# Maxima tasks in pairs at even distances, the first maxima rows through GpSimd's queue, and a second buffer for retrieved rows in a two-branch attention kernel

## Chip, core and metric

The kernel runs on one core of a Trainium2 chip. The metric is the device time of one execution in microseconds (us); the kernel before was run three times, and its median is 1981.27 us (1977.9 to 1982.19).

## The reference, cut to what matters

One input x of 2048 tokens and 512 features goes through two attention blocks of 32 heads of 16 columns each, and a gate mixes the two results.

```python
def _A_ref(x, wq, wk, wv, wo, beta):         # 4 segments of 512 tokens
    ...
    for s in range(N):
        qs, ks, vs = q[:, :, s], k[:, :, s], v[:, :, s]
        logits = einsum("bhqd,bhkd->bhqk", qs, ks) * scale + mask
        a_dot = einsum("bhqk,bhkd->bhqd", softmax(logits), vs)
        num = einsum("bhld,bhde->bhle", phi(qs), M)
        den = einsum("bhld,bhd->bhl", phi(qs), z)[..., None] + 1e-6
        outs.append(g * (num / den) + (1.0 - g) * a_dot)
        M = M + einsum("bhld,bhle->bhde", phi(ks), vs)
        z = z + einsum("bhld->bhd", phi(ks))
    ...
def _B_ref(x, wqkv, wo):                     # plain attention over all 2048 tokens
    ...
x = A_x
g = sigmoid((x * gate_w).sum(-1, keepdims=True))
return g * _A_ref(...) + (1 - g) * _B_ref(...)
```

Block A attends within a segment (its mask adds -1e9 where the key stands ahead of the query) and adds what a memory M, z of the earlier segments retrieves; block B has no mask.

## The kernel before

The program has a projection stage, an attention stage and a short tail. An attention unit is four heads and 512 queries; there are 32 units of B and 32 of A, and step k of the attention stage works on unit 32+k (B) and unit k (A) together.

**Projection.** Every product with a weight is a job of twelve 128x512 matmuls, because each operand is split into a high and a low part and three of the four products are kept. `qk_job` (L279) makes one 128-column group of Q or K for 512 tokens. ScalarE and VectorE split its PSUM bank into a tile `st` of four buffers (L286, L289), and two transfers store it to DRAM (L295). For block A, VectorE and ScalarE also make phi from the same bank (L285, L288, L291), so such a bank comes free only after the last of these. `v_job` (L262) makes V.

The part that the change touches is a loop over 16 blocks `blk`, group g and segment c of block A. A block runs two jobs of A (Q and K), then the memory of A: `mem_tr` transposes phi(K), `mem_upd` adds it to the state (L350, L358, L359), `mem_out` retrieves rows for Q, and `mem_put` transposes these and stores them. In between stand jobs of B from a list `fill`. From block 4 on these share four PSUM banks (`TB` twice, `MB`, `PVB`); another two (`SBK`, 128x1024 each) belong to the maxima.

**Retrieved rows.** `mem_out` copies two PSUM banks with ScalarE into a tile `om` (L314), VectorE scales it (L316 to L320), `mem_put` transposes it on TensorE (L327), ScalarE copies the result back into the same `om` (L329), and SyncE's queue stores it (L331). `om` has one buffer, so the next `mem_out` can't write it before that store has landed.

**Maxima.** The softmax subtracts a bound per query, which needs the maximum of the scores. `s_b` (B) and `s_a` (A) are maxima tasks. One is a pair of matmuls on the two 64-row halves of the array (L449 for B; L427 with mask matmuls L431 for A) into one of the two `SBK` buffers in turn, and one VectorE reduction of that buffer (L451; L435, L437). Unit 32 has 32 tasks and unit 0 six; these 38 are the list `first`. They are issued between the projection jobs by `spill()`, which is called after most pieces of a block. Blocks 4 to 13 each add 3.8 to a quota, and each call takes one task while the quota is at least 1, so a block's tasks stand behind its first pieces, one at a time. In block 14 the first six tasks of unit 33 (`EARLY`) follow in the same way; their keys have just been loaded into the space of x (tile `xh`, L148 and L369).

**From maxima to attention.** `m_chain(0)` (L460 to L470, VectorE) joins the maxima, `m_rows(0)` in block 15 transposes them (L476), ScalarE copies them to the tile `mr` (L478), and four small transfers (L484) write them into rows 48, 49, 112 and 113 of the query tiles of unit 32 (`qb`) and unit 0 (`qa`). The first score matmuls of the attention stage (L503, `t_group`) read these rows. The exponentials of L503's banks are L509, the products with V are L525. `m_rows` is called again in each step for the next units.

**Order.** Each engine runs its instructions in the order of the program. Nearly all transfers are issued by SyncE's queue (SP), one after another, and each waits there for its own data; weights and constant rows are issued by GpSimd's (POOL).

Of the kernel before, what the change touches and what calls it, by code (L numbers as in the profile page):

```python
# [7 lines left out]
FT = mybir.dt.float32  # L8
# [10 lines left out]
E = 16  # L19
# [8 lines left out]
S_FIRST = 10  # L28
S_LAST = 10
OMI = 14  # L30


@with_exitstack
def gated_mix_kernel(ctx, tc, x, wq, wk, wv, wo, beta, wqkv, wob, gate_w, out):
    nc = tc.nc
# [35 lines left out]
    X = proj.enter_context(tc.tile_pool(name="proj", bufs=1))  # L71
# [23 lines left out]
    def misc():  # L95
        return bank(mode["misc"])
# [48 lines left out]
    def set_aux(t, a, eng=None):  # L145
        n = t.shape[1] // 64
        for j in range(2):
            (eng or nc.gpsimd).dma_start(t.bitcast(FT)[64 * j + 48:64 * j + 64].rearrange("r (n t) -> r n t", n=n),  # L148
                                         aux[:, a, None, :].to_broadcast([E, n, 64]))
# [86 lines left out]
    def split_wv(k):  # L236
        split(WV[0][:, k, :], WV[1][:, k, :], WR.pop(k))
# [63 lines left out]
    def mem_state(g, c):  # L301
        return MST[c % 2][g % 2]

    def mem_out(g, c):
        m = mem_state(g, c)[:, :, :E + 1]
        o = X.tile([128, 4, 8, E], FT, name="om")
        r = X.tile([128, 4, 8], FT, name="recm")
        for n in range(2):
            b = misc()[:, :16 * (E + 1)].rearrange("p (i h e) -> p i h e", i=2, h=8)
            for i in range(2):  # L310
                nc.tensor.matmul(b[:, i], PHI[g, 0, c][:, (2 * n + i) * 128:(2 * n + i + 1) * 128], m,
                                 start=True, stop=True)
            nc.scalar.activation(r[:, 2 * n:2 * n + 2], b[:, :, :, E], AF.Copy)
            nc.scalar.activation(o[:, 2 * n:2 * n + 2].rearrange("p i h e -> p (i h) e"),  # L314
                                 b[:, :, :, :E].rearrange("p i h e -> p (i h) e"), AF.Copy)
        nc.vector.tensor_scalar(r, r, 1e-6, None, op0=OP.add)  # L316
        nc.vector.reciprocal(r, r)
        nc.vector.tensor_tensor(r, r, gate[:, 4 * c:4 * c + 4, None].to_broadcast([128, 4, 8]), op=OP.mult)
        o3 = o.rearrange("p i h e -> p (i h) e")
        nc.vector.tensor_tensor(o3, o3, r.rearrange("p i h -> p (i h)")[:, :, None].to_broadcast([128, 32, E]), op=OP.mult)  # L320
        PHI[g, "o", c] = o
# [53 lines left out]
    def q_of(u):  # L375
        return QA[u % 2] if u < 32 else QB[u % 3]
# [95 lines left out]
    def m_rows(k):  # L472
        m8 = M8.pop(k)
        b = misc()[0:64, :128]
        for a in range(2):
            nc.tensor.matmul(b[32 * a:32 * a + 32], m8[:, a], ident, start=True, stop=True)  # L476
        mr = W.tile([64, 128], FT, name="mr", bufs=1)
        nc.scalar.activation(mr, b, AF.Copy)  # L478
        for n, u in ((1, 32 + k if k < 32 else None), (0, (0, None)[k] if k < 2 else k - 1)):
            for a in range(2):  # L480
                if u is None:
                    continue
                r = 32 * a + 16 * n
                nc.sync.dma_start(q_of(u).bitcast(FT)[48 + a:128:64], mr[r:r + 16])  # L484

    PT = {}
    AT = {}
# [148 lines left out]
    ST_B = [(i, p, kc) for i in range(4) for p in range(2) for kc in range(4)]  # L636
    ST_A = [(3, 0), (3, 1), (2, 0), (2, 1), (1, None), (0, None)]

    def s_tasks(u):
        return [todo(s_a, u, *t) for t in ST_A] if u < 32 else [todo(s_b, u, *t) for t in ST_B]  # L640
# [60 lines left out]
    first = s_tasks(32) + s_tasks(0)  # L701
    st33 = [todo(s_b, 33, *t) for t in sorted(ST_B, key=lambda t: t[2])]
    early = st33[:EARLY]
# [6 lines left out]
    split_wv(2)  # L710
    nf = 0
    quota = 0

    def spill():
        nonlocal quota
        if quota >= 1:
            quota -= 1
            (first or early).pop(0)()

    S0 = [b[:, 0] for b in SBK]  # L720
    CUM = (2, 4, 6, 9, 11, 13, 16, 18, 20, 22, 24, 27, 29, 32, 34, 36)
    for blk in range(16):
        g, c = divmod(blk, 4)
        pg, pc = divmod(blk - 1, 4)
        if blk == 4:
            mode["misc"] = TB + [MB, PVB]
        if 4 <= blk < 14:
            quota += len(ST_A + ST_B) / 10
        if blk == 14:
            for p in range(2):  # L730
                set_aux(KB[1][:, p], 0, nc.sync)
            load_kb(1, 0)
        n = blk + 1 + (c == 2)
        if c < 3 and n < 16:
            load_vm(n // 4, n % 4)
        qk_job(0, "A", g, 0, c)
        if c == 3 and g < 3:
            split_w(0, "A", g + 1, (0,))
        spill()
        if blk == 0:  # L740
            split_wv(3)
            do_beta()
        if blk > 0:
            if pc == 0:
                mem_upd(pg, pc)
        qk_job(0, "A", g, 1, c)
        spill()
        if c == 2 and g < 3:
            load_w("A", g + 1)
        if c == 3 and g < 3:  # L750
            split_w(0, "A", g + 1, (1,))
        if blk == 4:
            load_q(33)
            load_ka(0)
            load_q(0)
            load_va(0)
        if blk == 6:
            load_w("B", 1)
        for f, n in ((store_gate, 5), (load_grow, 7), (do_grow, 10)):
            if blk == n:  # L760
                f()
        if blk == 14:
            m_chain(0)
        if blk == 15:
            m_rows(0)
        want = CUM[blk]
        mt = [[], [], []]
        if c > 0:
            mt[0] += [todo(mem_out, g, c)]
            mt[2] += [todo(mem_put, g, c)]  # L770
        if c < NC4 - 1:
            mt[1 + (c == 0)] += [todo(mem_tr, g, c)]
        for n in range(3):
            for f in mt[n]:
                f()
            if blk == 14 and n == 2:
                quota = EARLY
            if mt[n]:
                spill()
            if blk == 14:  # L780
                load_kb(1, 1 + n)
            if nf == 35:
                mode["misc"] = [MB, PVB, TB[1]]
            if nf < want:
                fill[nf]()
                spill()
                if nf in (18, 24):
                    load_w("B", 2 + nf // 24)
                if nf in (15, 20, 26):
                    split_w(2 if nf == 20 else 1, "B", nf // 5 - 2)  # L790
                nf += 1
        if blk == 13:
            for f in first:
                f()
            first, quota = [], 0
        if 0 < c < NC4 - 1:
            mem_upd(g, c)
        if blk == 14:
            spill()
        if blk == 15:  # L800
            for f in early:
                f()
        if nf >= 16 and "vb" not in AT:
            AT["vb"] = 1
            load_vb(0)
# [42 lines left out]
    def extras(k):  # L848
# [5 lines left out]
        post[2 * S_LAST + 4] = [todo(m_rows, k + 1)]  # L854
        for n, at in [(k - 9, 1)] + [(23, 2 * OMI)] * (k == 31):
            if n >= 0:
# [99 lines left out]
    for t in range(4):  # L956
        d = den[:, t * 128:(t + 1) * 128]
        o = o_cols(3, t)[:, 3, 0]
# [36 lines left out]
```

## Time and profile before

| what | value |
|---|---|
| median of three runs (lowest, highest) | 1981.27 us (1977.9, 1982.19) |
| profiled execution: span from first to last instruction | 1976.0 us |
| lowest run less this span, highest run less this span | 1.9 us, 6.2 us |
| TensorE busy | 1944.8 us, 98% |
| VectorE busy | 1630.3 us, 83% |
| ScalarE busy | 1435.7 us, 73% |
| GpSimd busy | 257.5 us, 13% |
| mean granted TensorE clock | 0.997 |

The page gives the profiled execution's span, not the time that a timed run of it would show; the two differ by what lies ahead of the first and behind the last instruction. A row of the timeline has the start in us, the length in us, the engine, the line, the operation, what is written <- what is read, the shape and the count of instructions merged into the row; in brackets stands how long the engine was idle before it and what ended that. PE is TensorE's matmuls, PEld its weight loads, DVE VectorE, ACT ScalarE, POOL GpSimd, SPq an issue by SyncE's queue. A row of the windows view has the stretch, its length, the busy us of each engine with instruction counts, the granted TensorE clock, the busy share of the transfer engines, and GB/s.

### The profile page before, as it was taken

Reading aid. Unit: us, or ns where it says so; the run is one execution under the profiler, and the core shown is the slowest. Engines: PE = TensorE matmul, PEld = TensorE weight load, DVE = VectorE, ACT = ScalarE, POOL = GpSimd, SP = SyncE. Lnnn points to the kernel's source line nnn. Section 1 sums busy time; section 2 is a strip of 40 time slices with the busy share of each in tenths; the row PEclk is TensorE's granted clock in tenths of the full one; section 3 lists DMA queues with packets and bytes.
Section 4 is the critical chain, followed back from the end, with each engine's and each line's share of the span. In section 5 each row is a group of like instructions: output and inputs, shape, how many; then the busy total and the mean of one; then the engine's idle time right before and its main releaser. Section 6 shows DMA issues by size and latency. Waiting matters only on the chain.

```text
span 1976.0 us, 43643 instructions
## 1 busy us (share of the span) xinstructions
PE 1944.8 (98%) x17517; PEld 945.6 (48%) x17517; DVE 1630.3 (83%) x1825; ACT 1435.7 (73%) x2703; POOL 257.5 (13%) x474
## 2 busy tenths in 40 slices
PE   8999999999999999999999999999999999999999
PEld 6887777434344344444444444444444444444435
DVE  6135665899999999999999999999999999999942
ACT  3233332688888888888888888888888888888884
POOL 2200000011210101111010101010101010101012
PEclk9999999999999999999999999999999999999999
DMA  6766656644443444344445353444344444444111
GB/s 205 172 209 183 191 186 173 152 111 114 97 114 88 103 86 103 86 114 86 114 85 112 86 113 86 114 86 114 86 108 91 96 102 87 102 90 103 48 51 57
DMA packets 162742, 222.49 MB, mean 113 GB/s; under 512 B 39260, under 2 KB 89452, under 8 KB 156780
## 3 DMA queue, kind: packets, MB, share of 16 engines
q1 hardware_dynamic: 159596, 211.70, 44.0%
q0 software_dynamic: 2944, 8.00, 2.1%
q8 instruction: 138, 2.26, 0.5%
q14 instruction: 64, 0.52, 0.1%
HBM read 148.21 MB, written 68.16 MB: 109 GB/s over the span
## 4 chain that ended last, share of the span: by engine, by line
PE 90%; DMA 3%; DVE 2%; ACT 2%; issue 1%; SPq 1%; ACTq 0%; DVEq 0%
PE pvb L525 31%; PE tb L503 17%; PE sbk L449 12%; PE mb L503 8%; PE tb L279 3%; PE tb L591 2%; PE mb L279 2%; PE sbk L427 2%; PE pvb L279 2%; PE tb L262 2%; DVE mxb L451 1%; ACT raw L509 1%; PE mb L591 1%; PE mb L262 1%; PE sbk L431 1%
## 5 line engine op out<-in xcount | busy, mean ns | idle before, releaser
L451 DVE TENSOR_REDUCE mxb<-sbk 128x2 f32<-128x1024 f32 x1024 | 1226.1, 1222 | 36.6 <-PE sbk L449 32.4
L509 ACT ACTIVATE raw<-tb 128x512 f32<-128x512 f32 x1557 | 888.2, 598 | 163.1 <-PE tb L503 90.7
L525 PE MATMUL pvb<-raw,vb 128*17 128x256 f32 (+1 forms) x8072 | 639.4, 388 | 0.0
L509 ACT ACTIVATE raw<-mb 128x512 f32<-128x512 f32 x780 | 466.4, 598 | 76.5 <-PE tb L503 44.8
L503 PE MATMUL tb<-qb,xh 64*128 64x512 f32 x872 | 330.8, 496 | 1.7 <-ACT raw L509 1.7
L525 PEld LDWEIGHTS pvb<-raw,vb 128*17 128x17 f32 x8072 | 134.4, 95 | 341.7 <-issue 336.6
L449 PE MATMUL sbk<-xh,qb 64*128 64x512 f32 x1344 | 283.1, 398 | 2.0 <-DMA xh<-dB 0.8
L503 PE MATMUL mb<-qb,xh 64*128 64x512 f32 x445 | 219.6, 494 | 0.0
L503 PEld LDWEIGHTS tb<-qb,xh 64*128 64x128 f32 x872 | 124.4, 183 | 188.1 <-issue 91.4
L512 POOL TENSOR_SCALAR_AFFINE_SELECT raw<-raw 128x256 f32<-128x256 f32 (+1 forms) x320 | 116.1, 363 | 700.1 <-ACT raw L509 692.3
L503 PE MATMUL tb<-qb,kb 64*128 64x512 f32 x471 | 176.3, 496 | 1.4 <-DMA qb<-mr 0.8
L435 DVE TENSOR_REDUCE mx<-sbk 128x2 f32<-128x768 f32 (+1 forms) x128 | 139.8, 1092 | 43.1 <-PE sbk L431 37.1
L449 PE MATMUL sbk<-kb,qb 64*128 64x512 f32 x704 | 150.6, 406 | 1.2 <-DVE mxb L451 1.1
L449 PEld LDWEIGHTS sbk<-xh,qb 64*128 64x128 f32 x1344 | 137.9, 186 | 7.3 <-DVE mxb L451 3.5
L503 PEld LDWEIGHTS mb<-qb,xh 64*128 64x128 f32 x445 | 81.3, 183 | 86.6 <-issue 48.0
L503 PE MATMUL mb<-qb,kb 64*128 64x512 f32 x233 | 115.4, 495 | 0.7 <-DVE st L289 0.7
L565 POOL TENSOR_TENSOR o<-o,d 128x512 f32<-128x512 f32 x31 | 39.8, 1283 | 562.6 <-DMA d<-rd 281.6
L503 PEld LDWEIGHTS tb<-qb,kb 64*128 64x128 f32 x471 | 66.0, 183 | 98.4 <-issue 52.5
L525 PE MATMUL pvb<-raw,va 128*17 128x256 f32 (+2 forms) x1280 | 94.7, 383 | 5.8 <-ACT pvs L534 5.8
L427 PE MATMUL sbk<-ka,qa 64*128 64x256 f32 (+3 forms) x512 | 86.8, 346 | 1.2 <-ACT raw L509 1.2
L503 PE MATMUL tb<-qa,ka 64*128 64x384 f32 (+3 forms) x340 | 79.2, 372 | 0.0
L449 PEld LDWEIGHTS sbk<-kb,qb 64*128 64x128 f32 x704 | 71.6, 185 | 12.6 <-issue 6.5
(273 smaller groups left out, 1790.7 us busy)
## 6 DMA issues: line engine op xcount, KB each, us to landing
xh<-dB SPq DMA_DIRECT2D x38, 512.0 KB
vb<-vdB SPq DMA_DIRECT2D x16, 1088.0 KB
dB<-st SPq DMA_DIRECT2D x64, 256.0 KB
dA<-st SPq DMA_DIRECT2D x64, 256.0 KB
pd<-pvs SPq DMA_DIRECT2D x64, 256.0 KB
kb<-dB SPq DMA_DIRECT2D x22, 512.0 KB
xh<-dB SPq DMA_DIRECT2D x38, 256.0 KB
qb<-dB SPq DMA_DIRECT2D x64, 128.0 KB
```

What stands on the lines that cost most here:

```text
L262: nc.tensor.matmul(b, lhs, WV[wi][:, k, :], start=n == 0, stop=n == 11)
L279: nc.tensor.matmul(b, WS[ws][w][wi][:, k, :], (XH, XL)[xi][c][:, k, :], start=n == 0, stop=n == 11)
L427: nc.tensor.matmul(b[:, j, c0:c0 + n], q_of(u)[r, p, i * 128:(i + 1) * 128], k_of(u, p)[r, :n], start=True, stop=False)
L435: nc.vector.tensor_reduce(m[:, :, p, i], b[:, :, :n], axis=AX.X, op=OP.max)
L449: nc.tensor.matmul(b[:, j], q_of(u)[r, p, i * 128:(i + 1) * 128], k_of(u, p)[r, kc * C:(kc + 1) * C], start=True, stop=True)
L451: nc.vector.tensor_reduce(MXB[u][:, :, p, i, kc], b, axis=AX.X, op=OP.max)
L503: nc.tensor.matmul(bs[j][:, c0:c0 + w], k_of(u, h // 2)[r, 128 * it:128 * it + 128], q_of(u)[r, h // 2, q0:], start=True, stop=True)
L509: nc.scalar.activation(pt, bs[j], AF.Exp, scale=SCALE)
L512: nc.gpsimd.affine_select(out=m, in_=m, pattern=[[1, 128]] if n < 2 else [[0, 2], [1, 128]], compare_op=OP.is_ge, fill=0.0, base=0, channe ...
L525: nc.tensor.matmul(PVB[32 * h:32 * h + E + 1, q0 + lo:q0 + hi], vt[:, it, 4 * q + h, :], pt[:, lo:hi], start=it == 0 and lo == 0, stop=it ...
L565: nc.gpsimd.tensor_tensor(o, o, d, op=OP.mult)
L591: nc.tensor.matmul(b, (AT["oh"], AT["ol"])[oi][:, g, a], (AT["wh"], AT["wl"])[wi][:, g, a], start=n == 0, stop=n == 11)
```

## The change

```diff
+SPILLS = 64
...
     def mem_out(g, c):
         m = mem_state(g, c)[:, :, :E + 1]
-        o = X.tile([128, 4, 8, E], FT, name="om")
+        o = X.tile([128, 4, 8, E], FT, name="om", bufs=2)
...
                 r = 32 * a + 16 * n
-                nc.sync.dma_start(q_of(u).bitcast(FT)[48 + a:128:64], mr[r:r + 16])
+                (nc.sync if k else nc.gpsimd).dma_start(q_of(u).bitcast(FT)[48 + a:128:64], mr[r:r + 16])
...
     quota = 0
+    rate = 0
 
     def spill():
         nonlocal quota
-        if quota >= 1:
-            quota -= 1
-            (first or early).pop(0)()
+        quota += rate
+        if quota >= 2:
+            quota -= 2
+            for _ in range(2):
+                (first or early).pop(0)()
...
-        if 4 <= blk < 14:
-            quota += len(ST_A + ST_B) / 10
+        rate = len(ST_A + ST_B) / SPILLS if 4 <= blk < 14 else 0
```

In blocks 4 to 13 every call of `spill()` now adds 38/64 of a task, and two tasks are issued together once the sum reaches 2. The six tasks of block 14 come two to a call. The four writes of `m_rows(0)` are issued by GpSimd's queue; later calls keep SyncE's. `om` has two buffers. Lines below the first added one shift by one (L449 of the kernel before is L450 here, and so on), those behind the new `spill()` by three or four.

What TensorE's queue holds in block 7 (the rows with `sbk` are maxima tasks, `ws` and `wv` are weights, `mst` is the memory state), first as it was:

```order
L449 MATMUL sbk_114<-kb_89,qb_70 128x512 x2
L279 MATMUL pvb<-xh_88,ws_101 128x512 x4
L279 MATMUL pvb<-xh_88,ws_102 128x512 x4
L279 MATMUL pvb<-xl_96,ws_101 128x512 x4
L449 MATMUL sbk_113<-kb_89,qb_70 128x512 x2
L311 MATMUL tb_109<-mst_108,phi_1522 128x136 x2
L311 MATMUL tb_110<-mst_108,phi_1522 128x136 x2
L449 MATMUL sbk_114<-kb_89,qb_70 128x512 x2
L279 MATMUL mb<-xh_87,wv_97 128x512 x8
L279 MATMUL mb<-xl_93,wv_97 128x512 x4
L449 MATMUL sbk_113<-kb_89,qb_70 128x512 x2
L279 MATMUL pvb<-xh_87,wv_98 128x512 x8
```

and the same jobs with the change:

```order
L450 MATMUL sbk_113<-kb_89,qb_70 128x512 x2
L450 MATMUL sbk_114<-kb_89,qb_70 128x512 x2
L280 MATMUL pvb<-xh_88,ws_101 128x512 x4
L280 MATMUL pvb<-xh_88,ws_102 128x512 x4
L280 MATMUL pvb<-xl_96,ws_101 128x512 x4
L312 MATMUL tb_109<-mst_108,phi_1519 128x136 x2
L312 MATMUL tb_110<-mst_108,phi_1519 128x136 x2
L280 MATMUL mb<-xh_87,wv_97 128x512 x8
L280 MATMUL mb<-xl_93,wv_97 128x512 x4
L450 MATMUL sbk_113<-kb_89,qb_70 128x512 x2
L450 MATMUL sbk_114<-kb_89,qb_70 128x512 x2
L280 MATMUL pvb<-xh_87,wv_98 128x512 x8
```

Four places with one task each have become two with two each, with the other work in its old order.

TensorE's queue from the end of block 14 into block 15 (unit 33's tasks; L350 is `mem_upd`, L476 the transposition of the maxima), before:

```order
L449 MATMUL sbk_113<-xh_87,qb_68 128x512 x2
L350 MATMUL tb_110<-vm,pk 128x136 x4
L449 MATMUL sbk_114<-xh_87,qb_68 128x512 x2
L279 MATMUL mb<-xh_88,ws_99 128x512 x4
L279 MATMUL mb<-xh_88,ws_100 128x512 x4
L279 MATMUL mb<-xl_96,ws_99 128x512 x4
L449 MATMUL sbk_113<-xh_87,qb_68 128x512 x2
L279 MATMUL pvb<-xh_88,ws_101 128x512 x4
L279 MATMUL pvb<-xh_88,ws_102 128x512 x4
L279 MATMUL pvb<-xl_96,ws_101 128x512 x4
L449 MATMUL sbk_114<-xh_87,qb_68 128x512 x2
L476 MATMUL tb_109<-ident,m_2436 32x128 x2
```

and with the change:

```order
L450 MATMUL sbk_113<-xh_87,qb_68 128x512 x2
L450 MATMUL sbk_114<-xh_87,qb_68 128x512 x2
L351 MATMUL tb_110<-vm,pk 128x136 x4
L450 MATMUL sbk_113<-xh_87,qb_68 128x512 x2
L450 MATMUL sbk_114<-xh_87,qb_68 128x512 x2
L280 MATMUL mb<-xh_88,ws_99 128x512 x4
L280 MATMUL mb<-xh_88,ws_100 128x512 x4
L280 MATMUL mb<-xl_96,ws_99 128x512 x4
L450 MATMUL sbk_113<-xh_87,qb_68 128x512 x2
L450 MATMUL sbk_114<-xh_87,qb_68 128x512 x2
L280 MATMUL pvb<-xh_88,ws_101 128x512 x4
L280 MATMUL pvb<-xh_88,ws_102 128x512 x4
```

Two tasks that stood behind L476 now stand ahead of it, four tasks stand around one short `mem_upd`, and two further single visits (behind L476 and behind the next job) are gone.

SyncE's queue in block 15 held the four writes of the maxima rows between stores of projections, before:

```order
L369 DMA xh_87<-dB_127 32x2x512 x2
L295 DMA dA_118<-st 8x16x512 x2
L295 DMA dA_122<-st 8x16x512 x2
L484 DMA qb_70<-mr 2x8x128 x2
L484 DMA qa_73<-mr 2x8x128 x2
L295 DMA dB_125<-st 8x16x512 x2
L295 DMA dB_129<-st 8x16x512 x2
```

and GpSimd's queue holds them with the change:

```order
L360 TENSOR_TENSOR mst_106<-mtmp,mst_108 128x8x17
L360 TENSOR_TENSOR mst_108<-mtmp,mst_106 128x8x17
L485 DMA qb_70<-mr 2x8x128 x2
L485 DMA qa_73<-mr 2x8x128 x2
L149 DMA xh_88<-aux 16x32x64 x4
L513 AFFINE_SELECT raw_86<-raw_86 128x128 x4
```

They now stand behind the last two memory updates, and the stores of block A and block B are neighbours in SyncE's queue.

## The prediction

> **What bounds the kernel now.** I read the page first, then the windows view by stage, the timeline where TensorE has gaps, and the waits.
>
> ```profile
> span 1976.0 us, 43643 instructions
> PE 90%; DMA 3%; DVE 2%; ACT 2%; issue 1%; SPq 1%; ACTq 0%; DVEq 0%
> 148.00:308.00 160.00, 159.27 (x774) 118.95 (x774) 101.39 (x148) 51.99 (x111) 9.34 (x14) 1.00 0.60 185
> 324.00:350.00 26.00, 21.34 (x91) 15.12 (x90) 13.32 (x18) 5.74 (x14) 0.45 (x1) 0.87 0.62 179
> 350.00:376.00 26.00, 24.52 (x160) 13.30 (x156) 18.78 (x18) 12.45 (x24) 2.55 (x4) 1.00 0.68 138
> ```
>
> The chain of waits is 90% TensorE. Blocks 4 to 13 are the stretch from 148 to 308 us: TensorE is busy for 159.3 of 160 us, VectorE for 101, so what TensorE does not have to do there is time won. In blocks 14 and 15 TensorE is idle for 4.7 of 26 us, and its clock averages 0.87. This is the timeline of that hole, then the windows with the clock (the column behind POOL's):
>
> ```profile
> 334.38 0.27 ACT L478 ACTIVATE mr<-tb 64x128 f32<-64x128 f32 x1 [0.19 <-PE tb L476]
> 335.44 0.50 SPq L331 DMA_DIRECT2D om<-om  x1
> 338.81 0.49 PE L449 MATMUL sbk<-xh,qb 64*128 64x512 f32 x2
> 341.86 0.38 ACT L314 ACTIVATE om<-tb 128x256 f32<-128x256 f32 x1 [6.65 <-DMA om<-om]
> 342.30 3.78 PE L279 MATMUL tb<-xh,wv 128*128 128x512 f32 x8 [3.00 <-ACT om L314]
> 344.02 2.58 SPq L484 DMA_DIRECT2D qb<-mr  x2
> 345.88 1.91 PE L279 MATMUL tb<-xl,wv 128*128 128x512 f32 x4
> 347.59 0.92 PE L327 MATMUL mb<-ident,om 128*128 128x128 f32 x4
> 349.33 0.50 PE L503 MATMUL tb<-qb,kb 64*128 64x512 f32 x2 [0.83 <-DMA qb<-mr]
> 335.00:340.00 5.00, 4.30 (x20) 2.81 (x19) 1.05 (x1) 0.18 (x1) 0.00 (x0) 1.00 0.73 211
> 340.00:345.00 5.00, 2.70 (x6) 2.15 (x7) 2.49 (x6) 1.23 (x4) 0.00 (x0) 0.64 0.64 189
> 345.00:350.00 5.00, 4.17 (x17) 3.01 (x15) 2.49 (x4) 1.42 (x3) 0.00 (x0) 0.68 0.44 139
> ```
>
> ScalarE wants to write the one `om` buffer, whose store was issued only at 335.44 and landed some 6 us later, so it stands for 6.65 us. TensorE's next job needs the bank that ScalarE holds and stands for 3.00 us. Then the granted clock falls. Then the maxima rows, ready at 334.65 (334.38 + 0.27) but issued at 344.02 behind other transfers, keep the first score matmul waiting for 0.83 us.
>
> **Part 1: pairs in blocks 4 to 13.** A maxima task runs on 64 rows of the array, the jobs around it on 128. What one visit costs:
>
> ```profile
> 58.00 2.02 PE L262 MATMUL sbk<-wv,xh 128*128 128x512 f32 x8
> 60.77 2.02 PE L262 MATMUL tb<-wv,xh 128*128 128x512 f32 x8
> 204.14 2.12 PE L279 MATMUL mb<-xh,wv 128*128 128x512 f32 x8
> 207.12 0.51 PE L449 MATMUL sbk<-kb,qb 64*128 64x512 f32 x2
> 207.55 2.12 PE L279 MATMUL pvb<-xh,wv 128*128 128x512 f32 x8
> 349.67 0.62 PE L449 MATMUL sbk<-xh,qb 64*128 64x512 f32 x4
> 350.22 2.12 PE L279 MATMUL mb<-xh,wv 128*128 128x512 f32 x8
> 353.54 0.40 PE L449 MATMUL sbk<-xh,qb 64*128 64x512 f32 x2
> ```
>
> Two jobs back to back stand 2.77 us apart (58.00, 60.77); with one visit between them 3.41 us (204.14, 207.55). A visit costs 0.64 us. The second task of a visit costs less: the double row at 349.67 is 0.62 long, a single one in the same surroundings 0.40, so 0.22 for the second. The bounds: at least 0.12 (from a double's start to the next job 0.55, from a single's 0.43), at most 0.43, as if the second paid all of a single's way to the next job. A merged visit thus saves 0.42, between 0.21 and 0.52. There are 38 tasks in 38 visits before and 19 pairs after; 19 × 0.40 = 7.6 us (I round down, since some visits stand beside short matmuls), bounds 4.0 and 9.9.
>
> ```profile
> PE pvb L262 <- DVE phi L291: 0.7, 1, 0.7
> PEld sbk L449: 5.3, 8
> PE sbk L449: 1.8, 3
> ```
>
> The first row is from TensorE's waits, the other two list who waited for the reduction L451. One of the visits stands in front of a wait that stays, on phi (0.7 us), so I take 0.4 off: **-7.2 us**. The second of two reductions comes 1.2 us later on VectorE than before. I cost this at nothing, because a bank is reused after about three jobs of 2.77 us, and because before, in the whole program, matmuls of L449 wait for the reduction only three times (1.8 us). If that cover is gone, each pair costs up to one reduction; that is the slower rival.
>
> **Part 2: the second `om` buffer.** Away go the 3.00 us and what the lower clock cost behind them: the job from 342.30 to 347.59 took 5.29 us instead of 2.77 (2.52 lost), its transposes 0.92 instead of 0.60 (0.32). That is **-5.8 us**. Bounds: 3.0, if a run of the kernel before keeps its clock there, and 5.8. The Trainium skill, "TensorE: Matmul & The Clock Gate", Part 1, says that the gate judges a free-running window of 3413 ns, so the same stall may or may not lose the clock from run to run. Our rows show it lost; by that rule some runs of the kernel before would lack those 2.8 us, and the sum below would be 1971.1.
>
> **Part 3: the maxima rows on GpSimd's queue.** The 0.83 us go (**-0.8 us**) if the rows land earlier than TensorE arrives.
>
> ```profile
> 327.24 0.45 POOL L359 TENSOR_TENSOR mst<-mtmp,mst 128x136 f32<-128x136 f32 x1 [15.43 <-DVE mtmp L358]
> 358.67 1.28 POOL L148 DMA_DIRECT2D xh<-aux  x2 [30.98 <-PE tb L279]
> L148 POOL DMA_DIRECT2D xh<-aux x4: 631/640/652, 358.7 to 372.3; - x4
> DMA to landing us min/median/max: 3.5/7.1/14.5
> ```
>
> GpSimd is idle for 31 us from 327.7 on, so nothing stands before the four issues, and behind them only L148, 20 us later, waits. The rows are copied at about 335.9 in the new order (334.65 and 1.2 for the wait in part 4). With 0.64 us each, the two that L503 needs are issued by 337.2. The landing of such transfers took 3.5 to 14.5 us over all of L148's rows; the same tiny writes on SyncE's queue, issued from 344.02, were landed by 349.33, at most 5.3 us from the first issue. I take that: 341.2 to 342.5. TensorE arrives at about 343.5 (below), so no wait; the upper end would cost 8 us. SyncE's queue is relieved of 3.8 us of issues (344.02 to 347.85), ahead of stores whose buffers nobody waits for then; I cost this at nothing.
>
> **Part 4: pairs in blocks 14 and 15.** Here tasks come close together:
>
> ```profile
> 324.93 0.70 PE L449 MATMUL sbk<-xh,qb 64*128 64x512 f32 x2 [0.84 <-DMA xh<-dB]
> 325.67 1.23 DVE L451 TENSOR_REDUCE mxb<-sbk 128x2 f32<-128x1024 f32 x1 [0.60 <-PE sbk L449]
> 326.68 0.49 PE L449 MATMUL sbk<-xh,qb 64*128 64x512 f32 x2
> 332.15 0.68 DVE L291 SCALAR_TENSOR_TENSOR phi<-mb,phi 128x512 f32<-128x512 f32 x1
> 335.82 2.13 PE L279 MATMUL pvb<-xh,wv 128*128 128x512 f32 x8
> ```
>
> Four tasks now stand around one `mem_upd`. The fourth needs the buffer of the second, whose reduction ends at 325.67 + 2 × 1.23 = 328.1. Without a wait it would start at 326.68 + 2 × 0.22 = 327.1: **+1.0 us**. Then L291 ends 1.4 us later than its 332.83, two reductions (2.45) follow it on VectorE, and only then the 0.69 us that free the bank `pvb`: 334.2 + 2.45 + 0.69 = 337.4. The next job wants that bank at 335.82 + 1.4 + 0.2 - 0.6 (the visit that is gone ahead of it) = 336.8: **+0.6 us**. Three visits fewer save 3 × 0.4, of which I count two (the third falls into that wait): **-0.8 us**. Arrival at L503: 349.33 - 5.8 - 0.8 + 1.0 + 0.6 - 0.8 = 343.5.
>
> **Sum:** -7.2 - 5.8 - 0.8 + 1.0 + 0.6 - 0.8 = -13.0 us, from the profiled execution's span of 1976.0 to 1963.0. The runs shown lie 1.9 to 6.2 us above this span and their median 5.3; with that, **1968.3 us**. Behind 350 us the attention stage has the same order as before and I let it move as a whole. With the bounds of visits and clock, the forecast's own range is 1963.5 to 1973.
>
> **The rivals.**
>
> *Late rows.* GpSimd's issue or landing is so slow that TensorE stands for the rows as it did for `om`, and the clock falls again (3.0 + 2.8): the gain of part 2 goes back, and 1974.1 us remain. For it: the 14.5 us landing. Against it: 0.64 us per issue at 358 us with VectorE busy. The Trainium skill, "SBUF — State Buffer", "SBUF: two separate sides", says that a GpSimd-issued transfer can't get its descriptors written while VectorE holds the shared port, 620 ns becoming 3100. By that figure, an estimate, four issues take 12 us; no row here shows such an issue.
>
> *Only the last blocks gain.* Leaving the 64-row mode costs little, or the transfers (185 GB/s in that stretch) set its pace, and ScalarE waits for store buffers instead. Then parts 2 to 4 remain: 1975.5 us. Against it: one such wait between 200 and 420 us, the first row here (the second is two reductions in a row, 2.36 us, for the last rival).
>
> ```profile
> ACT st L286 <- DMA dB<-st: 2.2, 1, 2.2
> 350.11 2.36 DVE L451 TENSOR_REDUCE mxb<-sbk 128x2 f32<-128x1024 f32 x2 [0.96 <-PE sbk L449]
> ```
>
> *Given back.* The first attention step is held by VectorE (18.8 of 26 us busy from 350, three reductions in a row) or by loads that don't come earlier, and absorbs the shift: 1981.
>
> *Slower.* VectorE is in order. A pair puts 2.36 us of reductions in one piece before the subtraction or the phi that frees a job's bank, and with four banks TensorE then stands for one reduction, 1.22 us, at each of the 22 pairs: +26.8 against 15 us saved by all parts, 1993 us. It decides from 0.7 us per pair on (15 / 22). For it: part 4 shows two such places. Against it: VectorE is free for a third of blocks 4 to 13.
>
> **How the numbers follow.** Forecast 0.56, late rows 0.12, only the last blocks 0.12, given back 0.08, slower 0.12. The first three hold 0.80 and reach from 1963.5 to 1977, which is the range. A measurement of this kernel tells some 0.2%, 4 us, from no change: faster than 1977.3 is the chance of the first three less a little for their upper ends, 0.79; same 0.10; slower 0.11.
>
> **What would show it.** Right: in the profile of the changed kernel, jobs with a pair between them stand about 3.6 us apart; the wait of L314 on the store of `om` is gone and the clock is 1.00 around 335 to 345 us; the writes of the rows stand in POOL's rows, and L503 starts some 13 us before 349.33 without a wait. Wrong: waits of projection jobs on L451 or L289 at many pairs, ScalarE waiting for stores at L286, L503 waiting for the rows, or an attention stage longer than the 1627 us from 349 to the end.

## The result, and the profile after

| | before | with the change |
|---|---|---|
| median of five runs each, on the same chip | 1981.65 us (1977.9 to 1982.19) | 1969.33 us (1964.77 to 1971.98) |
| ratio of the times, 95% interval | | 0.9938 (0.992 to 0.9956) |
| the same, five further runs of the change (eleven of before) | 1981.03 us | 1971.70 us, 0.9956 (0.9943 to 0.9969) |
| profiled execution, span | 1976.0 us | 1970.2 us |

The change makes the kernel faster, by 12.3 us in the first comparison and 9.3 in the second. The two profiled spans lie only 5.8 us apart. A timed run takes 1.8 us more than its own span (1971.98 for the span of 1970.2, 1964.77 for one of 1963.0), so the profiled execution of the change is the slowest of its five, and that of the kernel before, 1977.8 by the same offset, is as fast as its fastest. The profile therefore shows where time went, but only part of how much.

The page of the changed kernel, span and chain of waits:

```profile
span 1970.2 us, 43646 instructions
PE 91%; ACT 3%; DMA 2%; DVE 2%; issue 1%; SPq 1%; ACTq 0%; DVEq 0%
```

The bound is what it was, TensorE. The useful comparison is one of equal work, so I cut both traces at the same instructions: the third, eleventh and twelfth `mem_out` (the row groups of L311, L312 after the change) and the first score matmul (L503, L504). The columns are those of the windows view: stretch, length, busy us of TensorE's matmuls, its weight loads, VectorE, ScalarE and GpSimd with their counts, granted clock, transfer share, GB/s. Before:

```profile
135.40:316.46 181.06, 180.29 (x882) 135.67 (x882) 107.95 (x162) 57.88 (x124) 9.79 (x15) 1.00 0.60 184
316.46:334.27 17.81, 16.97 (x85) 12.63 (x85) 11.05 (x21) 5.80 (x13) 0.45 (x1) 1.00 0.61 150
334.27:349.33 15.06, 11.24 (x43) 8.21 (x41) 6.75 (x10) 2.97 (x8) 0.00 (x0) 0.77 0.63 186
349.33:1976.00 1626.67, 1610.14 (x15932) 686.58 (x15932) 1449.96 (x1515) 1323.57 (x2469) 221.21 (x403) 1.00 0.43 96
```

With the change:

```profile
134.56:309.94 175.38, 173.91 (x882) 135.60 (x882) 107.89 (x162) 57.39 (x124) 9.79 (x15) 1.00 0.60 188
309.94:331.87 21.93, 18.69 (x89) 13.90 (x89) 13.40 (x23) 5.44 (x13) 0.45 (x1) 0.92 0.60 157
331.87:339.75 7.88, 7.39 (x39) 5.91 (x37) 3.64 (x7) 2.32 (x8) 2.29 (x4) 1.00 0.64 182
339.75:1970.20 1630.45, 1613.96 (x15933) 689.54 (x15932) 1449.16 (x1516) 1324.31 (x2471) 221.26 (x403) 1.00 0.43 97
```

The first stretch holds the same 882 matmuls and is 5.68 us shorter: TensorE needs 6.38 us less for them and idles 0.70 more. The second is 4.12 us longer, the third 7.18 shorter with its clock back at 1.00. The attention stage is 3.78 us longer in this execution. From the third `mem_out` to the end that makes -5.0. The timeline of the changed kernel in the second and third stretch:

```profile
320.79 1.42 PE L450 MATMUL sbk<-xh,qb 64*128 64x512 f32 x4 [3.24 <-DMA xh<-dB]
331.47 0.90 SPq L332 DMA_DIRECT2D om<-om  x1
332.13 0.26 ACT L479 ACTIVATE mr<-tb 64x128 f32<-64x128 f32 x1
332.68 1.19 POOL L485 DMA_DIRECT2D qb<-mr  x2 [7.44 <-ACT mr L479]
332.72 0.38 ACT L315 ACTIVATE om<-tb 128x256 f32<-128x256 f32 x1
333.55 2.12 PE L280 MATMUL pvb<-xh,wv 128*128 128x512 f32 x8 [0.49 <-DVE st L290]
333.86 1.11 POOL L485 DMA_DIRECT2D qa<-mr  x2
339.75 0.50 PE L504 MATMUL tb<-qb,kb 64*128 64x512 f32 x1
347.76 3.56 PE L280 MATMUL tb<-xh,wv 128*128 128x512 f32 x8
```

L315 writes the second `om` 1.25 us after the store of the first was issued (331.47), without a wait. The rows are ready at 332.39 and issued at 332.68, and L504 starts without a wait. New are 3.24 us in which the first pair of unit 33 waits for its keys, and half-speed jobs (eight matmuls of 347.76 take 3.56 us, not 2.1). The records of the clock put its half-speed windows, each 3.41 us long, at 320.73, 348.04 and 1897.69 us.

### The profile page after: what moved, and what is told of

Same layout as the page of the kernel before. It is cut to its first block, busy times and chain, and to the rows that moved or that the text cites. A ratio compares the mean times of both kernels' runs of the same rounds, so it can differ in the third digit from the quotient of the medians.

```text
span 1970.2 us, 43646 instructions
## 1 busy us (share of the span) xinstructions
PE 1939.4 (98%) x17517; PEld 947.3 (48%) x17517; DVE 1628.8 (83%) x1825; ACT 1434.9 (73%) x2703; POOL 259.9 (13%) x478
## 4 chain that ended last, share of the span: by engine, by line
PE 91%; ACT 3%; DMA 2%; DVE 2%; issue 1%; SPq 1%; ACTq 0%; DVEq 0%
PE pvb L526 31%; PE tb L504 17%; PE sbk L450 12%; PE mb L504 8%; PE tb L280 3%; PE tb L592 2%; PE mb L280 2%; PE pvb L280 2%; PE tb L263 2%; PE sbk L428 2%; PE sbk L280 1%; ACT raw L510 1%; PE mb L592 1%; DVE mxb L452 1%; PE sbk L432 1%
## 5 line engine op out<-in xcount | busy, mean ns | idle before, releaser
L504 PE MATMUL tb<-qb,xh 64*128 64x512 f32 x872 | 330.8, 496 | 1.7 <-ACT raw L510 1.7
L450 PE MATMUL sbk<-xh,qb 64*128 64x512 f32 x1344 | 283.8, 398 | 4.1 <-DMA xh<-dB 3.2
L504 PE MATMUL mb<-qb,xh 64*128 64x512 f32 x445 | 219.9, 494 | 0.0
L504 PEld LDWEIGHTS tb<-qb,xh 64*128 64x128 f32 x872 | 124.3, 183 | 188.0 <-issue 91.6
L504 PE MATMUL tb<-qb,kb 64*128 64x512 f32 x471 | 177.1, 496 | 1.2 <-DVE st L290 0.6
L450 PE MATMUL sbk<-kb,qb 64*128 64x512 f32 x704 | 146.4, 401 | 0.7 <-DVE mxb L452 0.7
L450 PEld LDWEIGHTS sbk<-xh,qb 64*128 64x128 f32 x1344 | 138.3, 186 | 8.2 <-issue 3.8
L504 PEld LDWEIGHTS mb<-qb,xh 64*128 64x128 f32 x445 | 81.5, 183 | 87.2 <-issue 47.8
L504 PE MATMUL mb<-qb,kb 64*128 64x512 f32 x233 | 115.4, 495 | 0.8 <-DVE st L290 0.8
L504 PEld LDWEIGHTS tb<-qb,kb 64*128 64x128 f32 x471 | 66.3, 183 | 98.4 <-issue 53.5
L504 PE MATMUL tb<-qa,ka 64*128 64x384 f32 (+3 forms) x340 | 79.2, 372 | 0.0
L438 DVE TENSOR_REDUCE mx<-sbk 128x4 f32<-128x1024 f32 x64 | 61.0, 954 | 19.8 <-PE sbk L432 19.8
```

The source lines that it names most:

```text
L438: nc.vector.tensor_reduce(m[:, :, :, i], b.rearrange("q j (p k) -> q j p k", p=2)[:, :, :, :n], axis=AX.X, op=OP.max)
L450: nc.tensor.matmul(b[:, j], q_of(u)[r, p, i * 128:(i + 1) * 128], k_of(u, p)[r, kc * C:(kc + 1) * C], start=True, stop=True)
L504: nc.tensor.matmul(bs[j][:, c0:c0 + w], k_of(u, h // 2)[r, 128 * it:128 * it + 128], q_of(u)[r, h // 2, q0:], start=True, stop=True)
```

## Experiments

Each run was profiled and timed beside the kernel before. The table cuts each profile like the windows above: A from the third to the eleventh `mem_out`, B to the twelfth, C to the first score matmul, D to the end (us). The waits are TensorE's on the keys of unit 33 (in B), on `om` and on the maxima rows (in C). The runs of the kernel before had medians of 1981.96 us beside pairs alone, om alone, om and rows and singles; of 1980.83 beside rows alone, pairs and om, fours and constants on GpSimd; of 1981.03 beside the change again and the last two. "Before" and "the change" are the profiles shown above.

```
                        A       B      C      D     keys  om   rows  median   ratio (95%)
before               181.06  17.81  15.06  1626.7   0.8  3.0   0.8
pairs alone          175.35  18.82  14.14  1629.3   0.7  2.4   3.5   1974.41  0.9963 (0.9950-0.9976)
om alone             181.02  18.48  15.05  1630.8   1.4   -    6.6   1981.25  1.0001 (0.9987-1.0015)
rows alone           181.31  21.01  12.02  1627.0   2.5  2.0    -    1980.06  0.9988 (0.9979-0.9997)
om and rows          181.02  18.29   8.39  1629.2   1.3   -     -    1974.35  0.9968 (0.9957-0.9979)
pairs and om         175.34  20.39  13.38  1627.7   1.6   -    5.4   1977.18  0.9977 (0.9966-0.9988)
singles, even        181.58  18.31   8.38  1630.0   1.4   -     -    1976.41  0.9974 (0.9964-0.9984)
the change           175.38  21.93   7.88  1630.5   3.2   -     -    1969.33  0.9938 (0.9920-0.9956)
the change again     175.39  20.78   7.89  1629.6   2.6   -     -    1971.70  0.9956 (0.9943-0.9969)
constants on GpSimd  175.37  19.64   7.90  1629.3   1.5   -     -    1971.16  0.9950 (0.9937-0.9962)
last pairs later     175.35  18.45   7.54  1629.5   0.2   -    0.3   1970.77  0.9948 (0.9931-0.9964)
last pairs last      175.34  17.19   8.71  1626.9    -    -     -    1970.75  0.9946 (0.9934-0.9958)
fours                223.57  18.69   7.89  1628.7   0.5   -     -    2014.68  1.0178 (1.0163-1.0193)
```

**Pairs alone.** The kernel before with the changed `spill()`:

```diff
+        quota += rate
+        if quota >= 2:
+            quota -= 2
+            for _ in range(2):
+                (first or early).pop(0)()
...
+        rate = len(ST_A + ST_B) / SPILLS if 4 <= blk < 14 else 0
```

> The kernel before with the pairs alone (one om buffer, rows on SyncE's queue). If leaving and entering the 64-row mode is what pairs save: L312 of block 14, which stood at 316.45 us before and 309.93 with the whole change, stands near 310 here too, and the wait for the om store stays; the time is 4 to 7 us under the kernel before. If only the last blocks gain, L312 stays near 316 and the time is within 1 us of the kernel before. If pairs hold up TensorE, it is slower.

The median is 7.6 us below that of the kernel before beside it, a little more than expected, and A is as short as in the whole change, 5.7 us under the kernel before (the interval of the median is 4.8 to 9.9 us). L312 of block 14 stands at 314.51 us, neither near 310 nor near 316, because this execution came to the third `mem_out` 3.8 us later than the one before (139.16 against 135.40); counted from there it is 5.7 us earlier. TensorE's waits behind it:

```profile
PE tb L504 <- DMA qb<-mr: 3.5, 1, 3.5
PE tb L280 <- ACT om L315: 2.4, 1, 2.4
```

Both late transfers remain, and the one for the rows costs more than before. The gain of the pairs is made ahead of them and is kept.

**Even distances without pairs.** The whole change, but one task at a time:

```diff
-        if quota >= 2:
-            quota -= 2
-            for _ in range(2):
-                (first or early).pop(0)()
+        if quota >= 1:
+            quota -= 1
+            (first or early).pop(0)()
```

> The whole change, but the tasks one at a time at even distances (38/64 of a task per call, one issued when the sum reaches 1). If pairing is what saves: L312 of block 14 stands near 316 us and the time is that of the second buffer and the rows alone, some 7 us slower than the whole change. If even distances are what saves: the time of the whole change.

The first stretch of this kernel, in the windows view:

```profile
132.19:313.77 181.58, 180.37 (x881) 136.09 (x882) 108.32 (x162) 57.95 (x124) 9.76 (x15) 1.00 0.59 183
```

TensorE needs 180.37 us for the work that took it 180.29 before. The even distances are worth nothing; the shorter busy time is that of joining two tasks in one visit. Its time is that of "om and rows" (the intervals overlap), as it should be: 5.6 us under the kernel before beside it, where the change is 12.3 and 9.3 us under its own. Its L312 of block 14 stands at 313.77 us, in an execution that came to the third `mem_out` at 132.19.

**The second buffer alone.**

```diff
-        o = X.tile([128, 4, 8, E], FT, name="om")
+        o = X.tile([128, 4, 8, E], FT, name="om", bufs=2)
```

> The kernel before with the second om buffer alone. If the terms add as the prediction has them: 5.8 us faster (3.0 of stall, 2.8 of clock). If the second buffer only uncovers the next wait: the maxima rows are issued at 344 us by SyncE's queue as before and land at 349, so the first L503 still starts near 349, waiting some 5 us for the rows with the clock falling again, and the time is within 1.5 us of the kernel before.

No measurable change. The issue and the copy of the rows in the timeline of this kernel:

```profile
333.75 0.27 ACT L478 ACTIVATE mr<-tb 64x128 f32<-64x128 f32 x1 [0.18 <-PE tb L476]
343.71 2.74 SPq L484 DMA_DIRECT2D qb<-mr  x2
348.68 0.79 PE L503 MATMUL tb<-qb,kb 64*128 64x512 f32 x2 [6.59 <-DMA qb<-mr]
```

The wait on `om` is gone and TensorE reaches L503 at 342.09 (348.68 - 6.59). But the rows, ready at 334.02, are issued by SyncE's queue at 343.71, 9.7 us later, hardly earlier than before (344.02). In between the queue issues nine other transfers, which takes it 8.6 us (0.67 + 4.02 + 3.94):

```profile
334.84 0.67 SPq L331 DMA_DIRECT2D om<-om  x1
335.56 4.02 SPq L369 DMA_DIRECT2D xh<-dB  x4
339.68 3.94 SPq L295 DMA_DIRECT2D dA<-st  x4
```

All that the buffer gains is waited out at L503.

**The rows alone.**

```diff
-                nc.sync.dma_start(q_of(u).bitcast(FT)[48 + a:128:64], mr[r:r + 16])
+                (nc.sync if k else nc.gpsimd).dma_start(q_of(u).bitcast(FT)[48 + a:128:64], mr[r:r + 16])
```

> The kernel before with the four writes of the maxima rows on GpSimd's queue and nothing else. If the two late transfers stand one behind the other: the wait for the om store (3.0 us) and the low clock stay, the rows land long before L503 is reached, only the 0.8 us of waiting for them go, and the time is within 2 us of the kernel before. If the rows alone were what held the last blocks: some 6 us faster.

A gain of about 0.1% (0.9979 to 0.9997). C is 3.04 us shorter, but B in this execution longer by 3.20 (keys waited for and a half-speed window), ahead of anything that the edit touches, so B and C together are as long as before (33.0 and 32.9 us). The wait on `om` stays (2.0 us), and so does a half-speed window.

**Both together.** The two edits above in the kernel before.

> The kernel before with the second om buffer and the rows on GpSimd's queue, no pairs. If the last blocks gain as the prediction has it: no wait for om and none for the rows, 6.6 us faster. If transfers set the pace there: less than 3 us faster, with a wait on a landing near 340 to 350 us.

The median is again 7.6 us lower. The third stretch in the windows view, of the buffer alone, the rows alone, and both:

```profile
333.63:348.68 15.05, 8.46 (x42) 6.21 (x40) 6.77 (x10) 2.96 (x8) 0.00 (x0) 0.86 0.62 181
```

```profile
336.99:349.01 12.02, 10.01 (x43) 7.35 (x41) 6.06 (x9) 2.02 (x7) 2.29 (x4) 0.86 0.61 181
```

```profile
339.44:347.83 8.39, 8.39 (x42) 6.21 (x40) 6.08 (x9) 2.06 (x7) 2.28 (x4) 1.00 0.72 210
```

15.06 us before becomes 15.05, 12.02 and 8.39. The 3.0 us of the rows alone are no gain, since B lost as much: B and C together take 33.5, 33.0 and 26.7 us, against 32.9 before. With both, TensorE is busy throughout at full clock. The two late transfers stand one behind the other, and either hides the other's delay.

**Pairs and buffer**, the change with the rows back on SyncE's queue:

```diff
-                (nc.sync if k else nc.gpsimd).dma_start(q_of(u).bitcast(FT)[48 + a:128:64], mr[r:r + 16])
+                nc.sync.dma_start(q_of(u).bitcast(FT)[48 + a:128:64], mr[r:r + 16])
```

> The whole change with the rows back on SyncE's queue. If the second buffer is worth nothing without early rows: L503 waits 4 to 7 us for the rows, and the time is that of the pairs alone, some 7 us under the kernel before and 5 to 6 over the whole change. If the terms of the prediction add: 1 us over the whole change.

```profile
PE tb L504 <- DMA qb<-mr: 5.4, 1, 5.4
PE sbk L450 <- DMA xh<-dB: 1.6, 1, 1.6
```

The wait on the rows is back, 5.4 us, and C is 13.38. The median is 3.7 us under the kernel before beside it, half of what was expected, and 6.0 over "constants on GpSimd" of the same comparison, which has the rows on GpSimd's queue; its interval overlaps that of the pairs alone. The buffer without early rows is worth nothing here too. Inside the change the move to GpSimd's queue is thus worth 5.5 us of C (13.38 to 7.88). The Trainium skill, "DMA: Bandwidth & Descriptors", "Issuing engines are not separate DMA queues", says that starting transfers from several engines saves only the sequencer's time for starting them, which is usually small. Here that time was not small: issuing the transfers ahead of them held ready rows back for most of 9.7 us (the buffer alone, above), and another queue issued them 0.3 us after the copy.

**Fours in place of pairs**, in blocks 4 to 13 of the change, to see what decides a visit's cost when it grows:

```diff
-        if quota >= 2:
-            quota -= 2
-            for _ in range(2):
+        n = 4 if blk < 14 else 2
+        if quota >= n:
+            quota -= n
+            for _ in range(n):
```

> The whole change, but four tasks to a visit in blocks 4 to 13 (pairs as before in blocks 14 and 15). There are two SBK buffers. If a visit's cost is the change of the array's rows alone: nine visits fewer, 3.6 us faster than the whole change. If the reductions limit longer visits: the third and fourth task of a visit each wait about 1 us for a reduction of 1.22 us, nine or ten visits, and the time is 12 to 18 us over the whole change.

The median is 33.9 us above the kernel before beside it and 43.5 above "constants on GpSimd" of the same comparison, which differs from the change in one queue only. That is far more than the 12 to 18 us expected. It is all in A: 223.57 against 175.38, 48.2 us. TensorE and VectorE at two of its visits:

```profile
181.61 0.74 PE L450 MATMUL sbk<-kb,qb 64*128 64x512 f32 x4
185.55 0.58 PE L450 MATMUL sbk<-kb,qb 64*128 64x512 f32 x2 [3.20 <-DVE mxb L452]
186.68 0.80 PE L450 MATMUL sbk<-kb,qb 64*128 64x512 f32 x2 [0.55 <-DVE mxb L452]
189.22 3.67 PE L263 MATMUL tb<-wv,xh 128*128 128x512 f32 x8
208.44 0.49 PE L450 MATMUL sbk<-kb,qb 64*128 64x512 f32 x2 [3.81 <-DVE mxb L452]
```

```profile
183.68 0.68 DVE L292 SCALAR_TENSOR_TENSOR phi<-tb,phi 128x512 f32<-128x512 f32 x1
184.27 4.61 DVE L452 TENSOR_REDUCE mxb<-sbk 128x2 f32<-128x1024 f32 x4
```

The third task needs the buffer of the first. The matmuls of the first two tasks are over at 182.35 (181.61 + 0.74), but VectorE begins to reduce only at 184.27, behind the phi chain of the job ahead (L292), and the third task waits for 3.20 us. This agrees with the Trainium skill, "PSUM — Partial Sum Buffer", "Engine vs sequencer instructions", by which VectorE's queue is strictly first in, first out. The waits and the stretch as a whole:

```profile
PE sbk L450 <- DVE mxb L452: 29.9, 16, 3.8
```

```profile
132.73:356.30 223.57, 191.33 (x882) 148.17 (x882) 108.82 (x162) 57.61 (x124) 9.76 (x15) 0.91 0.49 149
```

29.9 us are these waits, 1.9 us each on average instead of the expected 1; another 17.4 us (191.33 - 173.91), which the expectation left out, is what the same 882 matmuls take longer at a mean clock of 0.91, in spite of fewer visits. Two tasks fill the two `SBK` buffers; from the third on a visit waits for VectorE's whole queue.

**The constants of the keys' tile on GpSimd's queue.** In the change B is longer. Is it SyncE's order, in which the four `set_aux` transfers stand ahead of the keys?

```diff
-                set_aux(KB[1][:, p], 0, nc.sync)
+                set_aux(KB[1][:, p], 0)
```

> The whole change with the four transfers of constant rows for the keys of unit 33 (L149 in block 14, each 1.0 to 2.4 us of issuing on SyncE's queue) issued by GpSimd. If SyncE's issue order is what makes the keys late: they are issued some 5 us earlier, the wait of TensorE for xh<-dB (3.2 us in the profile of the change) goes, and the time is 1 to 3 us under the whole change. If the transfer engines are full there: the keys land when they did and the time stays within 1 us.

The wait on the keys was 1.5 us in this execution, and the time cannot be told from the change. The first of the keys' four transfers is issued 4.5 us ahead of the eleventh `mem_out`, where in the run below it is issued 3.4 us behind it. But the four take 10.1 us to issue instead of 4.0, and TensorE has its keys 9.1 us behind that `mem_out` instead of 10.2. So an issue 7.9 us earlier brought the keys 1.1 us earlier; what holds these transfers back is not shown. Then I ran the **change again**, unedited:

> The whole change once more, beside the two that follow. If the wait for xh<-dB (3.2 us in the first profile of the change) comes from the order of issue, it is 2 us or more again; if it belongs to that one execution, it is near the 0.8 to 1.6 us of the other kernels. The time is 10 to 13 us under the kernel before.

Its second and third stretch, and TensorE's first two waits there:

```profile
310.97:331.75 20.78, 17.52 (x89) 12.92 (x89) 13.23 (x23) 5.44 (x13) 0.45 (x1) 1.00 0.60 156
331.75:339.64 7.89, 7.41 (x39) 5.93 (x37) 3.63 (x7) 2.31 (x8) 2.29 (x4) 1.00 0.73 195
```

```profile
PE sbk L450 <- DMA xh<-dB: 2.6, 1, 2.6
PE sbk L450 <- DVE mxb L452: 0.6, 1, 0.6
```

The keys are again late, 2.6 us, this time with the clock at 1.00. By the test set for this run that speaks for the order of issue, which the run with the constants on GpSimd's queue does not bear out. The table holds six executions with the pairs at this place (0.7, 1.6, 3.2, 2.6, 1.5 us, and 0.5 with fours; mean 1.7) and five with single tasks (0.8, 1.4, 2.5, 1.3, 1.4; mean 1.5). The two sets overlap, so it is not shown that the change makes this wait longer, and its cause stays open. The time is 9.3 us under the kernel before, a little less than expected.

**The last pairs later.** Two versions move the six tasks of unit 33. In the first the pairs stand behind `mem_upd` of block 14 and behind the two jobs after it; in the second behind those two jobs and the `mem_out` of block 15:

```diff
-            if blk == 14 and n == 2:
-                quota = EARLY
...
         if blk == 14:
+            quota = EARLY
             spill()
```

> The whole change with the three pairs of unit 33 issued one step later: behind mem_upd of block 14 and behind each of the two jobs that follow, so that no four tasks stand around mem_upd. If the crowd of four and the late keys cost TensorE time: the wait on the reduction goes, the wait for the keys shrinks by the 1.1 us of mem_upd, and the time is 1 to 3 us under the whole change. If that time is taken up behind it (store buffers, rows, keys of the next chunk): within 1 us.

```diff
-            if blk == 14 and n == 2:
-                quota = EARLY
...
         if blk == 14:
-            spill()
+            quota = EARLY
```

> The same one job later again: the pairs stand behind the two jobs of block 15 and behind mem_out. If late keys are what costs: no wait for xh<-dB at all, 2 to 4 us under the whole change. If the pair beside mem_out then holds the bank or the chain that L504 waits for: the gain of e10 or less.

The second and third stretch, of the first version and then of the second (work moves across the cut between B and C, so their sum counts):

```profile
312.33:330.78 18.45, 17.36 (x88) 12.89 (x89) 12.90 (x23) 5.79 (x13) 0.45 (x1) 1.00 0.57 148
330.78:338.32 7.54, 7.22 (x39) 5.90 (x37) 4.11 (x8) 2.47 (x8) 2.29 (x4) 1.00 0.77 208
```

```profile
315.06:332.25 17.19, 16.26 (x85) 12.29 (x85) 10.56 (x21) 5.79 (x13) 0.46 (x1) 1.00 0.59 154
332.25:340.96 8.71, 8.24 (x43) 6.29 (x41) 6.32 (x9) 2.07 (x7) 2.28 (x4) 1.00 0.70 198
```

The wait on the keys goes (0.2 and 0), and B and C together take 26.0 and 25.9 us, against 28.7 in the change again. Their medians, 1970.77 and 1970.75, lie 0.9 us under that run of the change and inside its interval, so the 1 to 3 and 2 to 4 us that late keys would have been worth did not show in the time. No version is shown to beat the change.

## Why the prediction was right, and where it was not

The forecast was 1968.3 us; the two medians of the change are 1969.33 and 1971.70. Direction, size and the likeliest case were right. That the first median lies within 1.0 us of the forecast is in part luck: up to the first score matmul the two profiles of the change are 8.7 and 9.9 us shorter than before, where 13.0 was forecast, and the second median is 9.3 us lower. Nor does the forecast's own range, "1963.5 to 1973", follow from its bounds: added up, those of the visits and of the clock give 1966.0 to 1974.7. The terms fared as follows.

**Pairs in blocks 4 to 13, -7.2 us: the mechanism is right, the gain smaller.** A measured 5.7, and "pairs alone" gained it alone. Where a visit stands between two long jobs it holds, as TensorE's timeline of the change shows:

```profile
206.95 2.11 PE L280 MATMUL tb<-xh,ws 128*128 128x512 f32 x8
209.91 0.74 PE L450 MATMUL sbk<-kb,qb 64*128 64x512 f32 x4
210.58 2.12 PE L280 MATMUL mb<-xh,ws 128*128 128x512 f32 x8
```

Job to job takes 3.63 us (210.58 - 206.95), as predicted, 0.22 over a single visit's 3.41. The price is near the predicted one over all visits too: from start to start in the two traces, less the same transitions without a visit and less waits, the 38 visits of A cost 24.9 us before and the 19 with the change 17.6, so 7.2 us or 0.38 for each merged visit. The prediction rounded down because some visits "stand beside short matmuls"; but those behind a short matmul saved 0.50 each and those behind a long one 0.39. Less came from unit 0's three pairs with their mask matmuls, 0.32 each. Of the 1.5 us between this 7.2 and the 5.7 of A, 0.6 are waits on VectorE: 0.9 us on phi, where 0.7 stood before, and 0.4 on the memory state (L356), which are new. The other 0.9 us, in the spacing of further matmuls, are not explained.

**Second buffer -5.8, rows -0.8: the sum is right, the split wrong.** Together -6.6 was predicted, and "om and rows" measured -6.67 in C. Alone the buffer gained 0.01 in C and nothing in time. The step that failed is "the 0.83 us go (-0.8 us)": it priced the rows by the wait that the profile showed, and that wait was small only because TensorE came late, held by `om`. The prediction itself had the numbers for it: arrival 5.8 us earlier against rows that on SyncE's queue would still land at 349. The 2.8 us for the clock were real in the profile of before, where the stall lost it.

**Pairs in blocks 14 and 15.** The bank `pvb` was predicted to cost 0.6 us and cost 0.49. The fourth task was predicted to wait 1.0 and waited 0.6 in three executions (the second row of waits of the change again is one); in the first profile of the change, where the clock was low behind the late keys, it did not wait. The wait on the keys, 0.84 us before, was left as it was. It measured 3.24 and 2.6 us with the change, and 0.7 to 2.5 in the kernels with a part of it; how much of that the earlier arrival of TensorE adds is not settled.

**The start of the first score matmul**, predicted "some 13 us before 349.33", is 339.75, 9.6 before (8.7 counted from the third `mem_out`). The change again has 9.9 by the latter count. By the stretches, A gave 1.5 us less than predicted, B cost 4.1 (3.0 in the change again) instead of some 0.6, and C gave 0.8 more.

**The attention stage** moved as a whole within what executions differ by: D lies between 1626.7 and 1630.8 us in all kernels, the one before with the least of them. The sign named for "given back", a stage longer than 1627 us, appeared (1630.45). In that execution two half-speed windows of 3.41 us would account for 3.4 of the 3.8 us, half of each being lost. But the change again has no such window there and still 1629.6, with 2.2 us more of idle TensorE than before, and "constants on GpSimd" has none and 1629.3; "last pairs last" has none either and 1626.9. Whether the stage gives 2 to 3 us of the gain back is not settled.

**From span to time.** "The runs shown lie 1.9 to 6.2 us above this span and their median 5.3" was taken for the distance of a median from its profile. It is 1.8 us for a run from its own span; the rest was the luck of the profiled execution. The sum went through all the same, since it was added to the median.

**The rivals.** "Late rows" fell: the four issues on GpSimd took 1.19 and 1.11 us by twos (332.68 and 333.86), and the rows were there. There was little to spare: they took 5.1 to 5.8 us to land, those of `qb` until about 339.0, and in "last pairs later" TensorE stood 0.3 us for them. "Only the last blocks gain" fell with "pairs alone", 0.9963. "Slower" was to come from VectorE's order, one reduction at each pair. With pairs TensorE waits for VectorE only twice in A, 0.9 and 0.4 us (0.7 us more idle time than before in all). With fours VectorE's order does make the kernel slower than before, but at another place than the rival named: no job waits for its bank there, the third task of a visit waits for its own buffer.

## What to carry to other kernels

When two late transfers stand one behind the other, the wait that a profile shows for the second is what the first leaves of it: price each by when its data would be there, and remove both, since here the larger removed alone gave nothing. Joining visits to a small array mode pays per visit until the visit needs more output buffers than there are; then it waits for the reader's whole queue. Before a difference of a few us is read from one profiled execution each, cut both traces at the same instructions and look how far other executions differ there.

## What the runs showed of the hardware that was not expected

**Half-speed windows lie on a grid of 3.41 us, and follow a stretch of it in which TensorE stood for much of the time.** In each of the thirteen executions the half-speed windows fit one grid; in the change those at 320.73 and 1897.69 us are 462 steps of 3.413 us apart. In blocks 14 and 15 every stall of TensorE of 3.0 us or more had one that began in it or within 2 us behind it (before 3.0, the change 3.24, pairs alone 3.5, pairs and `om` 5.4, `om` alone 6.6). Of those between 1.6 and 2.6 us three had one (2.5 and 2.0 in rows alone, 1.6 in pairs and `om`) and two had none (2.4 in pairs alone, 2.6 in the change again). Here are stretches of the grid of the change, then of the change again (behind the stretch stand its length and TensorE's busy time; the clock stands behind GpSimd's count):

```profile
317.32:320.73 3.41, 0.23 (x3) 0.00 (x0) 0.69 (x1) 1.05 (x2) 0.00 (x0) 1.00 0.56 138
1894.28:1897.69 3.41, 1.90 (x30) 0.82 (x28) 1.23 (x1) 2.85 (x5) 2.37 (x3) 1.00 0.14 41
1897.69:1901.10 3.41, 3.41 (x25) 1.80 (x24) 2.34 (x5) 0.93 (x2) 0.79 (x1) 0.50 0.03 14
```

```profile
316.33:319.74 3.41, 2.24 (x12) 1.63 (x10) 0.77 (x2) 1.18 (x2) 0.00 (x0) 1.00 0.56 131
319.74:323.15 3.41, 1.95 (x12) 1.52 (x12) 1.21 (x2) 0.00 (x0) 0.00 (x0) 1.00 0.53 162
```

The half-speed window at 1897.69 us has TensorE busy in all of it, but the stretch ahead of it only for 1.90 us; those at about 35 and 86 us, which some executions have, follow stretches with 29% to 48%. The stall of 2.6 us in the change again is shared by two stretches, each busy for more than half, and neither was followed by a half-speed window. Over the thirteen traces all 23 stretches at full clock with TensorE's matmuls busy for less than 46% were followed by one, and none of those busy for more than 67%; of the 46 between, 15 were and 31 were not, so the busy share alone is not the whole rule. The Trainium skill, "TensorE: Matmul & The Clock Gate", Part 1, has the clock fall after at least one idle window of about 3.4 us; the length of the windows agrees, but here stretches in which TensorE was busy for up to 66% of the time were followed by one too.

**The opening differs by execution.** The third `mem_out`, ahead of all that the change moves, starts between 132.2 us ("singles, even") and 140.1 us ("om and rows"). Three executions with half-speed windows at 35 and 86 us have it at 139.2 to 140.1; the rest of the spread has no cause shown.
